# An RWKV6 layer with an MLP on one core: the first round's tensors turned by overlapping transposes, evicted by two engines

## The chip, the core and the metric

The kernel runs on one core of a Trainium2 chip. A core has five engines that matter here: TensorE (PE; its weight loads are listed as PEld), VectorE (DVE), ScalarE (ACT), GpSimd (POOL) and SyncE (SP), which only issues DMAs in this kernel. Each engine works through its own list of instructions in order and waits on semaphores for the others. The metric is the time of one execution on the device in microseconds (us), lower is better. Several runs are made of each kernel, and the median is compared.

## What is computed

The reference, cut to what matters:

```
for t in range(S):                              # S = 768 steps, B = 4, H = 8, D = 48
    kt, vt, rt, wt = k[:, :, t], v[:, :, t], r[:, :, t], w[:, :, t]
    y[:, :, t] = einsum(rt, state + outer(u * kt, vt))
    state = wt[:, :, :, None] * state + outer(kt, vt)
x = y.transpose(0, 2, 1, 3).reshape(B, S, H * D)       # 4 x 768 x 384
xn = (x - mean(x)) / sqrt(var(x) + 1e-6) * g_ln
out = x + maximum(xn @ w_ch1, 0) @ w_ch2               # 384 -> 1536 -> 384
```

All data is float32.

## The kernel before

The 768 steps of each batch are cut into two halves of 384, so there are 8 rounds (4 batches x 2 halves). A round has two units, each of four heads (`u0`, `u1` in round 0; `new` are those of the next round). A unit needs `w`, `r` and `k` with the head dimension on the partitions, 64 rows to a head, two heads (a pair) to a tile of 128 x 384: that is what `turned` (line 306) makes. For the units of later rounds it does so with three 128 x 128 transposes and one eviction by ACT. For round 0 (line 318) the data is loaded in another layout (`load_rows`, line 133: 48 numbers of a head and a step block side by side, with zeros behind the last), and each 64 x 128 piece is made by a product with the identity; two of them, for the two heads of a pair, use the left and the right half of the array's columns.

`ps_t` holds two PSUM buffers, and every `turned`, `product_sums`, `ends` and `turned_x` takes one of them; so the third piece of work in a row waits until ACT has emptied the first. `products` (line 372) multiplies r by k, and `product_sums` (line 390) sums that over a head with six products against `sel`, which holds `u`; these have 2 moving columns each. `warm(n)` (line 292) puts products of zeros on PE, n x 128 columns; nobody uses their result, the profile calls them `idle`.

The decayed products inside a block of 64 steps are built by doubling: for each of six levels, `quads` (line 416) multiplies k and r on PE, 24 products a unit, `grow` (line 436) multiplies decays into k and r in place on DVE, and `keep` (line 453) writes the new part of A on DVE. A `grow` waits for the `quads` of its level, and the next `quads` for that `grow`. Behind the levels come the states (`ends`, `states`), the outputs (`own_outputs`, `outputs`), the layer norm (`moments`, `norm`, `turned_x`) and the MLP (`mlp`), whose products are interleaved with the levels of the next rounds.

The MLP's weights are converted in 24 parts: `begin` (line 243) is three ACT operations and the fetch of a further part by SP, `join` (line 284) is `shifted` and `added`, two and one DVE operations. The first three parts must be joined before the first product of the MLP.

The order is written out by hand: each engine's instructions stand in the order in which the program issues them (`InOrder`, line 39). The prologue, lines 734 to 818, is what the change touches: turn w, r, k of u0, with a `warm(2)` behind each; level 0 of u0; turn w of u1; totals; the sums of u0; turn r, k of u1; level 0 of u1; then the loop over levels 1 to 5 (line 769), in which the tensors of round 1 are turned along the way, with a `warm(3)` in levels 1 to 4.

Of the kernel before, what the change touches and what calls it, by code (L numbers as in the profile page):

```python
# [9 lines left out]
F32 = mybir.dt.float32  # L10
# [5 lines left out]
ALU = mybir.AluOpType  # L16
# [36 lines left out]
def kernel(  # L53
# [13 lines left out]
    PE, ACT, DVE, POOL, SPO = (  # L67
        InOrder(tc, e) for e in (nc.tensor, nc.scalar, nc.vector, nc.gpsimd, nc.sync)
    )
    SP = nc.sync  # L70

    B, H, S, D = r.shape
    P = 128
    HP = 64
# [4 lines left out]
    TT = 3  # L79
    RN = TT * P  # L80
# [3 lines left out]
    W = NK * P  # L84
    NLEV = 6
# [5 lines left out]
    pairs = range(NP)  # L91
# [4 lines left out]
    p2 = ctx.enter_context(tc.tile_pool(name="p2", bufs=2))  # L96
    p3 = ctx.enter_context(tc.tile_pool(name="p3", bufs=3))
# [24 lines left out]
    def load(q, which="wkr", eng=SP):  # L122
        for nm in which:
            for c in range(TT):
                eng.dma_start(
                    out=nat[nm][q % 2][:, c, :, 0:D],
                    in_=steps({"w": w, "k": k, "r": r}[nm], q, c),
                )

    def flat(nm, q):  # L130
        return nat[nm][q % 2].rearrange("p c h d -> p (c h d)")
# [33 lines left out]
    for j in range(2):  # L165
        ACT.dma_start(
            out=sel[ds(HP * j, D), :, j], in_=u.rearrange("(r j) d -> j d r", j=2)[j]
# [4 lines left out]
    ident = const.tile([P, P], F32, name="ident")  # L172
# [18 lines left out]
    for lev in range(NLEV - 1):  # L191
# [3 lines left out]
        for base, sign in ((0, 1), (n - 1, -1)):  # L195
            POOL.affine_select(
                out=m, in_=m, compare_op=ALU.is_ge, fill=0.0, base=base,
# [10 lines left out]
        out=bits0, in0=masks[0].rearrange("p q n -> p (q n)"), scalar1=-1.0, scalar2=None,  # L208
# [34 lines left out]
    def begin():  # L243
        nonlocal begun
        i = begun
        if i < len(parts) and i - joined < (len(held) if i < len(held) + LOW else LOW):
            words = raw.pop(i)
            lo, hi = words[:, :, 0].bitcast(U32), words[:, :, 1].bitcast(F32)
            if i < len(held):
                rest[i] = held[i].bitcast(I32)  # L250
            else:
                rest[i] = low.tile([P, WC], I32, tag="rest", name=f"rest{i}")
            upper = rest[i].bitcast(F16).rearrange("p (n two) -> p n two", two=2)[:, :, 1]
            ACT.activation(out=parts[i][0], in_=hi, func=AF.Abs, scale=2.0**-16)
            ACT.activation(out=rest[i], in_=lo, func=AF.Copy, scale=2.0**-29)
            ACT.activation(out=upper, in_=hi, func=AF.Copy, scale=2.0**-100)
            begun = i + 1
            fetch()
# [25 lines left out]
    def join():  # L284
        shifted()
        added()
# [5 lines left out]
    def warm(n, tag="m"):  # L292

        while n > 0:
            m = min(n, RN // P)
            ps = (ps_m if tag == "m" else ps_t).tile([P, RN], F32, tag=tag, name="idle")
            PE.matmul(
                ps[:, 0 : m * P], nought.broadcast_to([P, P]), nought.broadcast_to([P, m * P]),
                start=True, stop=True,
            )  # L300
            n -= m
# [4 lines left out]
    def turned(q, nm, pr):  # L306
        a = st.setdefault(q, {})
        if pr == 0:
            if nm == "w":
                if q % U == 0:  # L310
                    st["w"] = p1.tile([P, U, W], F32, tag="w", name=f"wT{q // U}")
                a["w"] = st["w"][:, q % U]
            elif "rk" not in a:

                rk = a["rk"] = p4.tile([P, 2, W], F32, tag="rkT", name=f"rkT{q}")
                a["r"], a["k"] = rk[:, 0], rk[:, 1]
        ps = ps_t.tile([P, RN], F32, tag="t", name=f"{nm}_ps{q}_{pr}")
        if q < U:

            for c in range(TT):  # L320
                for j in range(2):
                    at = ((2 * pr + j) * TT + c) * D
                    PE.matmul(
                        ps[ds(HP * j, HP), ts(c, P)], flat(nm, q)[:, ds(at, HP)], ident,
                        start=True, stop=True,
                    )
            ACT.copy(
                out=a[nm][:, ts(pr, RN)].rearrange("p (m c) -> p m c", c=TT),
                in_=ps.rearrange("p (c m) -> p m c", c=TT),
            )  # L330
            return
        for c in range(TT):
            PE.transpose(
                ps[:, ts(c, P)],
                nat[nm][q % 2][:, c, ts(pr, 2)].rearrange("p j d -> p (j d)"), ident,
            )
        ACT.copy(out=a[nm][:, ts(pr, RN)], in_=ps)
# [33 lines left out]

    def products(q, eng=DVE):
        a = st[q]
        if q < U:

            a["ruk"] = [
                p3.tile([P, RN], F32, tag="xn", name=f"ruk{q}_{pr}") for pr in pairs
            ]
            for pr in pairs:
                eng.tensor_tensor(  # L380
                    out=a["ruk"][pr], in0=a["r"][:, ts(pr, RN)], in1=a["k"][:, ts(pr, RN)],
                    op=ALU.mult,
                )
        else:
            ruk = p2.tile([P, NK, P], F32, tag="kn", name=f"ruk{q}")
            ruk = ruk.rearrange("p k t -> p (k t)")
            a["ruk"] = [ruk[:, ts(pr, RN)] for pr in pairs]
            eng.tensor_tensor(out=ruk, in0=a["r"], in1=a["k"], op=ALU.mult)

    def product_sums(q):  # L390
        b, f, g = units[q]
        a = st[q]
        ps = ps_t.tile([P, RN], F32, tag="t", name=f"own_ps{q}")
        for pr in pairs:
            for c in range(TT):
                PE.matmul(
                    ps[:, ts(pr * TT + c, 2)], a["ruk"][pr][:, ts(c, P)],
                    sel[:, NP * g + pr], start=True, stop=True,
                )
        o = a["own"] = p4.tile([P, TT, NH], F32, tag="own", name=f"own{q}")  # L400
        ACT.copy(
            out=o.rearrange("p c (r j) -> p r c j", j=2),
            in_=ps[:, 0 : 2 * NK].rearrange("p (r c j) -> p r c j", r=NP, j=2),
        )
# [11 lines left out]
    def quads(q, lev):  # L416

        n = 1 << lev
        rnd, uu = divmod(q, U)
        if uu == 0:  # L420
            ps = ps_a.tile([P, 2, 512], F32, tag="a", name=f"a_ps{rnd}_{lev}")
            a_ps[rnd] = ps[:, :, 0 : W // 2].rearrange("s j (u k t) -> s j u k t", u=U, k=NK)
        K = st[q]["k"]
        R = st[q]["r"].rearrange("p (m q two n) -> p m q two n", m=NM, two=2, n=n)
        for c in range(NK):
            for i in range(2):
                for j in range(2):
                    m = 2 * c + i
                    rows = ds(HP * j, D)
                    PE.matmul(  # L430
                        a_ps[rnd][ds(C * (i ^ j), C), j, uu, c]
                        .rearrange("s (q n) -> s q n", n=n),
                        K[rows, ts(m, C)], R[rows, m, :, 1, :], start=True, stop=True,
                    )
# [280 lines left out]
    def each(f, *ranges):  # L715
        calls = [()]
        for r_ in ranges:
            calls = [c + (x,) for c in calls for x in r_]
        return [lambda c=c: f(*c) for c in calls]

    def run(tasks):
        for t in tasks:
            t()
# [12 lines left out]
    fetch(2)  # L736
    for nm in "wrk":
        run(each(turned, [u0], nm, pairs))
        warm(2)
    for nm in "wrk":  # L740
        POOL.memset(nat[nm][0][:, :, :, D:HP], 0.0)
    products(u0)
    quads(u0, 0)
    load(new[0], "wrk", SPO)
    grow(u0, 0)
    run(each(turned, [u1], "w", pairs))
    totals(0, DVE)
    warm(2)
    product_sums(u0)
    for nm in "rk":  # L750
        run(each(turned, [u1], nm, pairs))
        warm(2)
    for nm in "wrk":
        POOL.memset(nat[nm][1][:, :, :, D:HP], 0.0)
    products(u1)
# [3 lines left out]
    load_v(u0, SPO)  # L759
    load(new[1], "r", SPO)  # L760
    load_v(u1, SPO)
    load(new[1], "k", SPO)
    begin()
    begin()
    warm(3)
    grow(u1, 0)
    keep(0, 0)
    ahead = each(turned, new[:1], "wrk", pairs) + each(turned, new[1:], "wrk", pairs)
    for lev in range(1, NLEV):
        quads(u0, lev)  # L770
        quads(u1, lev)
        run(ahead[2 * lev - 2 : 2 * lev] if lev < NLEV - 1 else [])
        if lev in (2, 3):
            begin()
        warm(3 if lev < NLEV - 1 else 0)
        for which in ("rk",) if lev < NLEV - 1 else "kr":
            for q in (u0, u1):
                grow(q, lev, which)
        keep(0, lev)
# [11 lines left out]
    exchanged(u0)  # L791
    states(u1)
    product_sums(u1)
    join()
    own_term(u1, POOL)
    own_outputs(u0)
    warm(3, "t")
# [4 lines left out]
    own_outputs(u1, "m")  # L802
    outputs(u1)
    moments(0)
    begin()
    load(units_of(2)[0], "w", SPO)
    load(units_of(2)[1], "w", SPO)
    run(ahead[8:])
# [3 lines left out]
    warm(3)  # L812
    norm(0)
    begin()
    join()
    products(new[1])
    run(each(turned_x, [0], range(KC)))
# [11 lines left out]
    for rnd in range(1, NR + 1):  # L829
# [3 lines left out]
        for lev in range(NLEV):  # L833
# [22 lines left out]
            if rnd == 1:  # L856
                if lev < 2:
                    tasks += each(load, new, "kr"[lev], [SPO])
                if lev == 2:
                    SPO.dma_start(  # L860
                        out=u_bc,
# [108 lines left out]
```

## Time and profile before

| | |
|---|---|
| median of 5 runs | 586.85 us (586.53 to 591.17) |
| the profiled execution | 586.53 us, of which 584.5 us are the profile's span |
| PE busy | 572.4 us (98%), 8644 instructions |
| DVE busy | 272.6 us (47%) |
| ACT busy | 195.0 us (33%) |
| POOL busy | 90.5 us (15%) |

The profile's page lists, for one execution, the busy time of the engines (part 1), the same in 40 slices of some 14.6 us with the clock that PE was granted in tenths of full speed (part 2), and the chain of work that ended last (part 4). Answers of the trace go further: busy time in any stretch, the chain in order of time, and the instructions in order of time. A group such as `x24` holds 24 records; a float32 product leaves two records, a transpose one. A busy PE is not PE at its peak, and idle products count as busy.

### The profile page before, as it was taken

To read this page: it belongs to the slowest core of one execution; us is meant where nothing else is said; L and a number is where in the kernel's file an instruction comes from. 1 tells how busy PE (TensorE), PEld (TensorE's weight loads), DVE (VectorE), ACT (ScalarE), POOL (GpSimd) and SP (SyncE) were. 2 spreads that over 40 slices of the span, in tenths; PEclk is the share of its full clock that TensorE was granted. 3 is DMA by queue.
4 is the path that set the end of the run, shared out by engine and by line. 5 is a ranking of instruction groups with operands and counts; after the bars stand their busy time and mean duration, and the time that the engine had idled before them with its cause. 6 is when DMAs were issued, how large, how long until landed. Compare 5 with 4: busy or idle time off the path is not lost.

```text
span 584.5 us, 19224 instructions
## 1 busy us (share of the span) xinstructions
PE 572.4 (98%) x8644; PEld 383.9 (66%) x8644; DVE 272.6 (47%) x575; ACT 195.0 (33%) x426; POOL 90.5 (15%) x124
## 2 busy tenths in 40 slices
PE   9998999999999999999999999999999999999997
PEld 6776765766666666666766666666666666666554
DVE  3889799687273634343462543336254531130000
ACT  3568586412442224311432124312331015202200
POOL 6130010204340025000620008000320000000000
PEclk9999899999999999999999999999999999999999
DMA  9928895037304311340204302031000000000000
GB/s 231 187 90 169 184 246 137 6 87 137 72 14 100 73 33 25 63 91 20 57 4 91 66 29 42 2 64 28 15 3 2 15 29 2 1 15 28 0 15 27
DMA packets 114193, 36.53 MB, mean 63 GB/s; under 512 B 104768, under 2 KB 111040, under 8 KB 114112
## 3 DMA queue, kind: packets, MB, share of 16 engines
q1 hardware_dynamic: 112240, 34.72, 27.1%
q8 instruction: 68, 1.11, 0.8%
q10 hardware_dynamic: 1872, 0.59, 0.4%
q14 instruction: 13, 0.11, 0.1%
HBM read 28.51 MB, written 4.72 MB: 57 GB/s over the span
## 4 chain that ended last, share of the span: by engine, by line
PE 92%; DVE 4%; ACT 3%; issue 1%; DVEq 0%; ACTq 0%
PE o_ps L49 32%; PE h_ps L49 31%; PE a_ps L49 11%; PE y L49 4%; PE w_ps L49 2%; PE k_ps L49 2%; PE kv L49 2%; PE idle L49 2%; PE r_ps L49 2%; PE kn_ps L49 2%; PE xT_ps L49 1%; DVE w_sb L49 1%; DVE rkT L49 1%; ACT rest L49 1%; PE own_ps L49 1%
## 5 line engine op out<-in xcount | busy, mean ns | idle before, releaser
L49 PE MATMUL o_ps<-w_sb,h 128*128 128x384 f32 x576 | 199.3, 490 | 1.3 <-ACT h L49 1.0
L49 PE MATMUL h_ps<-xT,w_sb 128*128 128x384 f32 x576 | 198.3, 492 | 0.0
L49 PEld LDWEIGHTS h_ps<-xT,w_sb 128*128 128x128 f32 x576 | 105.4, 191 | 62.5 <-issue 0.5
L49 PEld LDWEIGHTS o_ps<-w_sb,h 128*128 128x128 f32 x576 | 104.3, 190 | 62.7 <-ACT h L49 2.0
L49 ACT ACTIVATE h<-h_ps 128x384 f32<-128x384 f32 x96 | 46.9, 489 | 143.8 <-PE h_ps L49 143.7
L49 DVE TENSOR_TENSOR rkT<-rkT,tot 128x768 f32<-128x768 f32 (+1 forms) x96 | 76.6, 840 | 37.2 <-issue 26.0
L49 PEld LDWEIGHTS a_ps<-rkT 48*64 48x64 f32 x4608 | 72.0, 135 | 20.8 <-issue 14.7
L49 PE MATMUL a_ps<-rkT 48*64 48x32 f32 x4608 | 77.1, 220 | 0.3 <-issue 0.3
L49 DVE TENSOR_TENSOR o<-o_ps,x 128x384 f32<-128x384 f32 x24 | 13.4, 557 | 122.4 <-PE o_ps L49 122.3
L49 POOL TENSOR_TENSOR vo<-v,own 128x576 f32<-128x576 f32 x16 | 19.2, 1198 | 289.8 <-DVE own L49 249.8
L49 DVE SCALAR_TENSOR_TENSOR s<-s,decay,kv 128x48 f32<-128x48 f32 x160 | 29.3, 258 | 34.3 <-PE kv L49 34.2
L49 DVE COPY_PREDICATED A<-mask,a_ps 128x768 f32<-128x768 int8 x32 | 38.3, 1198 | 0.0
L49 DVE TENSOR_TENSOR x<-y,vo 128x288 f32<-128x288 f32 x32 | 13.1, 452 | 51.8 <-PE y L49 51.8
L49 ACT COPY rkT<-k_ps 128x384 f32<-128x384 f32 x32 | 14.3, 478 | 55.5 <-PE k_ps L49 55.5
L49 ACT ACTIVATE xT<-xT_ps,g_sb 128x384 f32<-128x384 f32 x24 | 13.6, 580 | 54.0 <-PE xT_ps L49 54.0
L49 ACT COPY rkT<-r_ps 128x384 f32<-128x384 f32 x32 | 14.6, 478 | 23.7 <-PE r_ps L49 23.7
L49 DVE TENSOR_SCALAR w_sb<-w_sb 128x384 f32<-128x384 f32 (+1 forms) x48 | 19.2, 401 | 0.8
L49 ACT COPY wT<-w_ps 128x384 f32<-128x384 f32 x32 | 14.4, 479 | 14.0 <-PE w_ps L49 8.9
L49 DVE TENSOR_REDUCE own<-rk 128x12 f32<-128x576 f32 x12 | 9.0, 750 | 20.7 <-POOL rk L49 20.6
L49 ACT ACTIVATE rstd<-mv,eps 128x3 f32<-128x3 f32 x8 | 2.4, 297 | 48.5 <-DVE mv L49 48.4
L49 DVE TENSOR_TENSOR rkT<-rkT,wT 128x768 f32<-128x768 f32 x16 | 17.8, 1146 | 0.8 <-PE a_ps L49 0.8
L49 PE MATMUL r_ps<-ident,nat_r 128*128 128x128 f32 (+1 forms) x132 | 16.2, 277 | 2.0 <-ACT rkT L49 1.9
(73 smaller groups left out, 520.3 us busy)
## 6 DMA issues: line engine op xcount, KB each, us to landing
raw<-in_moe_w_ch_dram SPq DMA_DIRECT2D x24, 384.0 KB, 4.0
v<-in_v_dram SPq DMA_DIRECT2D x48, 96.0 KB, 3.5
out_dram<-o SPq DMA_DIRECT2D x24, 192.0 KB, 2.5
nat_w<-in_w_dram SPq DMA_DIRECT2D x42, 96.0 KB, 3.4
nat_r<-in_r_dram SPq DMA_DIRECT2D x42, 96.0 KB, 2.9
nat_k<-in_k_dram SPq DMA_DIRECT2D x42, 96.0 KB, 2.8
vx<-v SPq DMA_DIRECT2D x28, 72.0 KB, 2.9
nat_r<-in_r_dram ACTq DMA_DIRECT2D x2, 288.0 KB, 5.0
```

What stands on the lines that cost most here:

```text
L49: return lambda *args, **kw: self.tc.keep_in_program_order(f(*args, **kw))
```

## The change

Five things change, all in round 0.

1. `turned` for round 0 uses PE transposes in place of products with the identity. For each block of steps and each pair it makes first a transpose of 128 columns, of which the upper 64 rows are wanted, and then one of 64 columns over the lower 64 rows, which the first had filled with other data.
2. For unit u0, the second pair's eviction goes to DVE in place of ACT.
3. `products` of round 0 is one DVE operation a unit in place of two, in a buffer of another pool.
4. All the `warm(2)` of the prologue go. The sums of u0 (`product_sums(u0)`) move from behind the totals to level 1 of the loop, where they take the place of `warm(3)`. The turning of u1's w moves ahead of u0's level 0.
5. A `begin` moves from behind `moments(0)` to level 4 of the loop; a `join` moves from ahead of u1's own term to behind the norm; the load of one k moves behind two `begin`s on SP.

```
         if q < U:
             for c in range(TT):
-                for j in range(2):
-                    at = ((2 * pr + j) * TT + c) * D
-                    PE.matmul(
-                        ps[ds(HP * j, HP), ts(c, P)], flat(nm, q)[:, ds(at, HP)], ident,
-                        start=True, stop=True,
+                for j in (1, 0):
+                    at = ((2 * pr + j) * TT + c) * D - HP * j
+                    PE.transpose(
+                        ps[0 : HP * (j + 1), ts(c, P)],
+                        flat(nm, q)[:, ds(at, HP * (j + 1))], ident,
                     )
-            ACT.copy(
+            (DVE.tensor_copy if q == 0 and pr else ACT.copy)(
...
     for nm in "wrk":
         run(each(turned, [u0], nm, pairs))
-        warm(2)
...
     products(u0)
+    load(new[0], "wrk", SPO)
+    run(each(turned, [u1], "w", pairs))
     quads(u0, 0)
-    load(new[0], "wrk", SPO)
     grow(u0, 0)
-    run(each(turned, [u1], "w", pairs))
     totals(0, DVE)
-    warm(2)
-    product_sums(u0)
-    for nm in "rk":
-        run(each(turned, [u1], nm, pairs))
-        warm(2)
+    run(each(turned, [u1], "rk", pairs))
...
-    load(new[1], "k", SPO)
     begin()
     begin()
+    load(new[1], "k", SPO)
...
-        if lev in (2, 3):
+        if lev in (2, 3, 4):
             begin()
-        warm(3 if lev < NLEV - 1 else 0)
+        if lev == 1:
+            product_sums(u0)
+        elif lev < NLEV - 1:
+            warm(3)
...
     product_sums(u1)
-    join()
     own_term(u1, POOL)
...
     moments(0)
-    begin()
     load(units_of(2)[0], "w", SPO)
...
     norm(0)
     begin()
     join()
+    join()
     products(new[1])
```

More of the change, by code (lines that the diff above doesn't have):

```diff
@@ L374, in products @@
         if q < U:
[L376 to L383, printed above, removed]
+            ruk = p2.tile([P, TT, H, D], F32, tag="x", name=f"ruk{q}")
+            ruk = ruk.rearrange("p c h d -> p (c h d)")[:, 0:W]
         else:
@@ L386, in products @@
             ruk = ruk.rearrange("p k t -> p (k t)")
-            a["ruk"] = [ruk[:, ts(pr, RN)] for pr in pairs]
-            eng.tensor_tensor(out=ruk, in0=a["r"], in1=a["k"], op=ALU.mult)
+        a["ruk"] = [ruk[:, ts(pr, RN)] for pr in pairs]
+        eng.tensor_tensor(out=ruk, in0=a["r"], in1=a["k"], op=ALU.mult)
     def product_sums(q):
```

## The prediction

> **What bounds the kernel now.** I read the chain in order of time first. For the first 24 us it is PE alone:
>
> ```profile
> 0.99 3.78 PE idle L49 x6
> 4.77 2.15 PE w_ps L49 x24
> 6.92 0.63 PE idle L49 x2
> 7.55 1.46 PE r_ps L49 x24
> 9.01 0.63 PE idle L49 x2
> 9.64 1.46 PE k_ps L49 x24
> 11.11 0.63 PE idle L49 x2
> 11.73 0.83 PE a_ps L49 x48
> ```
>
> No eviction and no DMA stands between the pieces, although r and k each wait for ACT by the program: the idle product covers the wait, or makes it. So a tensor costs 2.09 us (7.55 to 9.64), of which idle products take 0.63. Then I cut the span into stages (columns: stretch, PE busy, PEld, DVE, ACT, POOL, granted clock, DMA):
>
> ```profile
> 4.70:21.68 16.98, 16.98 (x268) 13.58 (x267) 6.44 (x12) 8.86 (x19) 6.60 (x27) 1.00 1.22 247
> 21.68:36.20 14.52, 14.11 (x513) 11.43 (x513) 13.34 (x15) 7.92 (x17) 1.63 (x2) 1.00 0.68 167
> 36.20:52.40 16.20, 14.04 (x418) 11.54 (x419) 15.45 (x53) 13.05 (x29) 5.88 (x7) 1.00 0.37 82
> 52.40:73.13 20.73, 20.73 (x242) 14.56 (x242) 17.48 (x34) 13.90 (x32) 0.00 (x0) 0.92 0.93 188
> 73.13:94.35 21.22, 18.79 (x292) 12.16 (x284) 19.81 (x35) 19.16 (x43) 2.45 (x2) 1.00 0.92 238
> ```
>
> Turning (row 1) is PE's; the levels (row 2) belong to PE and DVE about equally; states and norm are DVE's; row 4 is PE's again; row 5 is DVE's and ACT's. Behind 94 us the chain is PE's products, which the change doesn't touch. The change lies in rows 1 to 3, and what it saves must pass rows 4 and 5.
>
> Row 4 has a clock of 0.92. One stretch makes it:
>
> ```profile
> 60.77:64.19 3.42, 3.42 (x26) 3.07 (x27) 3.35 (x7) 0.34 (x2) 0.00 (x0) 1.00 1.11 275
> 64.19:67.60 3.41, 3.41 (x11) 2.30 (x10) 3.13 (x6) 1.00 (x3) 0.00 (x0) 0.50 1.19 142
> ```
>
> Asked for the sums' product alone, the first of these stretches holds
>
> ```profile
> 60.77:64.19 3.42, 2.56 (x23) 2.47 (x23) 0.34 (x2) 1.00 1.11 275
> ```
>
> So a 3.41 us window that was mostly sums (2 moving columns, "busy" while their weights load) is followed by one at half clock. By record starts, data streamed through the array for about 0.28 of it. The lowest other window, 43.71 to 47.12, has 0.53 (0.34 without transposes), and kept the clock.
>
> **The turning, on PE.** Before: 24 records a tensor, two side by side, 0.109 us a pair by their starts: 12 x 0.109 = 1.31. After: 12 transposes a tensor, one record each, none side by side. The near row is
>
> ```profile
> 23.31 0.87 PE L49 MATMUL w_ps<-ident,nat_w 128*128 128x128 f32 x6
> ```
>
> six in 0.87 with the last one's tail of 0.27 less 0.109, so 0.109 each: again 1.31. The transposes themselves gain nothing; the dropped idle products do.
>
> [...] The trace has its price: wherever 64-column products follow 128-column ones or the reverse, the start comes 0.095 us late (an idle of 0.213 us of streaming started at 9.26, the next k at 9.57; 25 of 25 switches from o_ps to a_ps are within 0.003 of it). The new code alternates 128 and 64 columns. [...] I take 0.109 and keep 0.205 as the other end.
>
> **The evictions.** ACT's take 0.478 (rows of wT and rkT). DVE's of this shape isn't in the trace: its copy of 32 x 384 from PSUM took 0.55, the low end; one DVE row took 1.88 in place of 0.99 while POOL copied, and POOL makes masks until 10.9 us, so 1.0 is the high end. I take 0.55, nearest in size. From the last start to an eviction is 0.35. A buffer's cycle is then 0.6 + 0.35 + 0.48 = 1.43 (DVE 1.50), just over PE's 1.31: evictions set the pace, at about 1.45 a tensor.
>
> In steps: w0 starts at 4.6, when the 8 first idle products end (its DMA landed at 4.40); its first eviction can't start before 6.63, when ACT's table is loaded; r0 from 7.1, k0 8.55, u1's w 10.0 to 11.5, u0's quads to 12.4, r1 from 12.5, k1 13.9, its evictions end at 16.0; before it was 20.0. On DVE: u0's products 10.8 to 11.7, grow from 12.5, totals (2.65) to 16.2, u1's products (0.96 in one, before 1.21 in two) to 17.1, grow to 18.0. Before, that grow ended at 21.93. **Gain 3.9.** With evictions of 1.0 it is 3.1. DMAs don't stop it: r0, k0, u1's tensors had landed by 4.8, 6.1 and 8.6, and round 1's w and r by 12.8 and 15.8, needed at 19 and 22. SP issues in the same order up to two fetches; the moved k load waits behind them (some 1 us) and is needed only behind 40 us.
>
> **Level 1.** Sums (12 x 0.111 = 1.34) take the place of warm(3) (0.65): PE's step from 3.08 to 3.75, plus one switch. DVE there is 0.8 us behind PE because of the 1.88 row, so part is covered; in levels 4 and 5 DVE waits for PE (0.79 at 32.5). **Cost 0.4**, bounds 0 and 0.75. Their eviction on ACT is 0.17, behind w's. The products' new buffers are those of x, which is first written at 45 us, when u0's sums have long been read: nothing.
>
> **The moved begin and join.** A begin is 1.7 us of ACT. From 45.92 to 47.46 PE waited for ACT, which was in two begins ahead of r's evictions; one is gone, PE gains 1.5 there. At level 4 it lies in ACT's idle (ACT 7.92 of 14.52), ahead of kn's eviction, which was released 0.5 us after it could have ended; if that cover is gone it costs up to 0.5. The join (1.25 of DVE) isn't saved: it moves from 43.2 to behind the norm. The norm comes some 1.3 earlier, the last of three joins ends at about 52.1 as it did (52.2). The first h product then starts at 51.5 relative to before, in place of 52.4, with the third part joined before its third weight is needed. **Gain 0.9**, bounds 0 and 1.3. PE carries it to 73 us, where DVE had been idle for 2.5 us.
>
> Sum without the clock: 3.9 - 0.4 + 0.9 = **4.4 us**.
>
> **The clock.** Where a low window falls depends on 3.41 us steps, counted from the rise at 6.16 us in this profile (product starts halve their distance there). In level 1 the new order runs 1.4 us of sums, then quads that stream 0.45 of their time: the window 19.8 to 23.2 comes to about 0.31, between the lost 0.28 and the kept 0.53. I think it is lost (chance 0.65). Half clock for 3.41 us is 1.7 us of PE; DVE covers a little: **cost 1.2**. Then the shift is 3.2 us, u0's and u1's later sums start at 57.3, and fall into the window 57.35 to 60.77: that loss stays. If level 1 keeps the clock, the shift of 4.4 splits those sums over two windows, and 1.5 more is gained.
>
> [...] The second is a narrow fit; I give it 0.17. [...]
>
> **The rivals.**
> - Likeliest (0.45): 4.4 - 1.2 = 3.2 from the profiled execution's 586.53, 583.3. The median of the runs shown is 0.3 above that execution, within noise; I put 583.3.
> - Clock kept in level 1, and later sums split (0.20): 4.4 + 1.5 = 5.9, 580.6.
> - Switches paid (0.10): w0 ends 7.7, each tensor 2.46, k1's last eviction 21.5 against 20.0: costs 1.5 + 0.4, gains 0.9, 587.5. [...]
> - Evictions slow, cover lost at kn, no gain at the norm (0.10): 3.1 - 0.75 - 0.5 - 1.2 = 0.7, 585.9.
> - The other side: transposes don't count (0.15). [...]
>
> A measurement of this kernel tells from no change what exceeds about 0.5%, 2.9 us. Faster by that: most of the first case, the second: 0.56. Within: the rest of the first, switches, slow evictions, the mild form of the last: 0.29. Slower: 0.15. The range from 579.8 to 588.5 leaves out the fastest ends of the second case and the last one.
>
> **What would show it.** Starts of the transposes 0.109 apart (0.205: switches; 0.213: half clock). k1's eviction done near 16, u1's first grow near 18. A half-clock row at about 23 to 27, and at 61 to 64. The first h product 4 to 5 us earlier than 52.4. The forecast is wrong if the clock falls before 16 us, if DVE's evictions take 1 us, or if the gain at 52 is gone at 94.

## The result, and the profile after

The changed kernel takes 586.49 us in the median of 43 runs (582.6 to 589.5), the kernel before 588.38 in 80 runs beside it (584.65 to 593.32). The ratio is 0.9961, 95% interval 0.9946 to 0.9976: faster by 0.4%, some 2.3 us by the ratio and 1.9 by the medians, where the prediction had 583.3 us. The profiled execution of the changed kernel took 588.74 us, of which 587.0 are the span.

**The prologue is as predicted.** This is the chain in order of time (columns: start, duration, what) in the changed kernel, from the second tensor on:

```profile
7.22 1.53 PE r_ps L49 x12
8.75 1.53 PE k_ps L49 x12
10.28 1.53 PE w_ps L49 x12
11.80 0.83 PE a_ps L49 x48
12.63 1.46 PE r_ps L49 x12
14.09 1.46 PE k_ps L49 x12
15.55 0.02 issue
15.57 0.49 ACT rkT L49
```

No idle product stands between the tensors; one follows the other after 1.53 us on the chain where it was 2.09, and k's last eviction ends at 16.06 (predicted: near 16.0). By the starts the transposes are 0.109 us apart. The first u1 `grow` on VectorE ends at 18.2, where before it was 21.93.

**Then the lead is lost.** Here are stretches of the changed kernel, cut at the same events as those of before (columns: stretch, PE, PEld, DVE, ACT, POOL busy, granted clock, DMA share, GB/s):

```profile
4.60:18.10 13.50, 12.39 (x216) 10.14 (x218) 7.75 (x13) 7.70 (x16) 6.66 (x28) 1.00 1.24 270
18.10:36.24 18.14, 17.90 (x460) 14.83 (x455) 12.82 (x14) 8.80 (x20) 1.53 (x2) 0.72 0.74 163
36.24:52.36 16.12, 15.03 (x461) 12.34 (x454) 14.35 (x51) 12.31 (x27) 5.87 (x7) 1.00 0.40 93
52.36:75.73 23.37, 23.37 (x276) 16.43 (x274) 19.61 (x39) 15.22 (x36) 0.00 (x0) 0.85 0.76 180
75.73:94.15 18.42, 17.17 (x245) 10.95 (x244) 17.05 (x32) 15.95 (x35) 2.31 (x2) 1.00 0.81 226
```

The turning has become 3.5 us shorter (16.98 to 13.50), but the levels took 18.14 us where before they took 14.52, at a mean clock of 0.72. The stretch from the first h product on took 23.37 in place of 20.73, at 0.85 in place of 0.92. In this profile the granted clock stays the same for 17.07 us from its first rise, then for 10.24, 30.72 and 6.83: five, three, nine and two times 3.41. Steps of 3.41 us from that rise are called windows here. Cut by them, the same kernel shows:

```profile
18.44:21.86 3.42, 3.18 (x82) 2.89 (x79) 3.42 (x4) 1.66 (x5) 0.00 (x0) 1.00 0.78 115
21.86:25.27 3.41, 3.41 (x101) 3.35 (x94) 2.62 (x4) 0.18 (x2) 1.53 (x2) 0.50 0.93 169
25.27:28.69 3.42, 3.42 (x70) 2.34 (x71) 1.05 (x3) 2.34 (x5) 0.00 (x0) 0.50 0.99 281
28.69:32.10 3.41, 3.41 (x48) 2.59 (x44) 2.63 (x3) 1.33 (x4) 0.00 (x0) 0.50 0.67 164
59.40:62.82 3.42, 3.42 (x100) 3.38 (x94) 3.21 (x10) 2.39 (x6) 0.00 (x0) 1.00 0.90 222
62.82:69.64 6.82, 6.82 (x19) 4.59 (x19) 6.48 (x11) 1.96 (x5) 0.00 (x0) 0.50 0.60 135
```

The clock falls where the prediction put it, behind a window that holds u0's sums, and again behind one with the later sums. But the first drop lasts three windows, 10.24 us, and the second two, where the prediction had counted one each. The sums' own share of the two windows in which the clock was lost is read by asking for their product alone:

```profile
18.44:21.86 3.42, 1.50 (x12) 1.41 (x12) 0.12 (x1) 1.00 0.78 115
59.40:62.82 3.42, 2.36 (x21) 2.36 (x22) 0.17 (x1) 1.00 0.90 222
```

PE counts as busy for 3.18 and 3.42 us of these windows. Worked out from each record's columns, at the 0.109 us of 128 of them, data streamed through the array for 0.37 and 0.23 of them only.

Once the clock is down, the levels are TensorE's alone. This is the chain through two of them at half clock and into the first at full clock:

```profile
21.70 2.57 PE a_ps L49 x96
24.27 1.47 PE r_ps L49 x6
25.75 1.28 PE idle L49 x2
27.03 2.72 PE a_ps L49 x96
29.74 1.47 PE k_ps L49 x6
31.21 1.15 PE idle L49 x2
32.36 1.53 PE a_ps L49 x96
```

A level takes 5.33 us there (21.70 to 27.03, 27.03 to 32.36) and 2.98 behind it (32.36 to 35.34). TensorE has no pause in these windows; it is VectorE that waits for it, 2.37 us ahead of one `grow`. But the `quads` stream for only 0.78 and 0.66 of their time in these two levels, where the turning and the idle product behind the first stream for 0.94.

**How many windows are lost differs from run to run.** Each run has its granted clock (to three digits) and span, so the number of windows at half clock, the lost windows, follows: (1 - clock) x span / 0.5 / 3.41, rounded. The first rise of the clock, from which the windows are counted, came at 6.16 us in the profile of before and at 4.79 in that of the changed kernel, so the same code falls into windows in different ways. Mean times in us by that number (runs in brackets; before: the runs taken beside the experiments, which have their clocks on record; rows of five and more left out):

| half-clock windows | before | after | before less after |
|---|---|---|---|
| 0 | 586.4 (2) | 583.1 (5) | 3.3 |
| 1 | 587.0 (22) | 584.4 (1) | 2.6 |
| 2 | 588.9 (21) | 585.0 (9) | 3.8 |
| 3 | 589.9 (15) | 586.1 (8) | 3.8 |
| 4 | 591.8 (14) | 587.7 (13) | 4.1 |
| all, with mean number | 589.2, 2.3 (77) | 586.5, 3.1 (44) | 2.7 |

At equal numbers of lost windows the changed kernel is about 3.9 us faster (the rows with eight runs or more on both sides). It loses 0.8 windows more than the kernel before, at 1.2 (after) to 1.5 us (before) each: 3.9 less 1.1 is 2.8, and the means show 2.7. The runs in the two columns weren't taken together, and the kernel before itself differs by some 0.5 us between one set of runs and another at equal numbers, so the 3.9 is good to about half a microsecond. And the profiled execution of before, from which all was reckoned, was one of those with a single window, 586.53 us against a mean of 589.2.

### The profile page after: what moved, and what is told of

It reads as the page before. It is cut to its first block, busy times and chain, and to the rows that moved or that the text cites. A ratio compares the mean times of both kernels' runs of the same rounds, so it can differ in the third digit from the quotient of the medians.

```text
span 587.0 us, 19053 instructions
## 1 busy us (share of the span) xinstructions
PE 574.6 (98%) x8558; PEld 385.8 (66%) x8558; DVE 272.1 (46%) x576; ACT 193.9 (33%) x423; POOL 91.8 (16%) x124
## 3 DMA queue, kind: packets, MB, share of 16 engines
q1 hardware_dynamic: 112240, 34.72, 26.4%
## 4 chain that ended last, share of the span: by engine, by line
PE 91%; ACT 5%; DVE 2%; issue 1%; DMA 1%; ACTq 0%; DVEq 0%
PE o_ps L49 32%; PE h_ps L49 30%; PE a_ps L49 11%; PE y L49 4%; PE kv L49 2%; PE k_ps L49 2%; PE r_ps L49 2%; PE w_ps L49 2%; PE kn_ps L49 2%; ACT rest L49 2%; PE xT_ps L49 1%; PE own_ps L49 1%; ACT rkT L49 1%; PE idle L49 1%; DVE w_sb L49 1%
## 5 line engine op out<-in xcount | busy, mean ns | idle before, releaser
L49 PEld LDWEIGHTS a_ps<-rkT 48*64 48x64 f32 x4608 | 74.1, 138 | 20.8 <-issue 14.0
L49 PE MATMUL a_ps<-rkT 48*64 48x32 f32 x4608 | 79.3, 222 | 0.1
L49 PE MATMUL r_ps<-ident,nat_r 128*128 128x128 f32 x108 | 16.7, 285 | 2.5 <-ACT rkT L49 1.5
L49 PEld LDWEIGHTS r_ps<-ident,nat_r 128*128 128x128 f32 x108 | 13.0, 142 | 8.1 <-issue 2.4
```

Of the source, the lines that this page charges most:

```text
L49: return lambda *args, **kw: self.tc.keep_in_program_order(f(*args, **kw))
```

## The experiments

Three theories were set against each other. CLOCK: the windows thinned out by the sums cost the gain, by their number. WORK: the change moved TensorE's work to where it is the bound, and what it won ahead of VectorE and ScalarE they don't carry on. FETCH came up with the first results: pauses of TensorE that no wait explains, at fixed places of its instruction list. The experiments were measured in four sets, each with the kernel before beside it: 589.94 us in the first (e1, e3, e4, e5), 588.65 in the second (e6 to e9), 588.64 in the third (e10 to e12), 588.97 in the last. At one, two and three lost windows the kernel before is 0.2, 0.7 and 0.4 us longer in the first set than in the second, so a difference of some 0.5 us between kernels of these two sets isn't shown.

**e1: u0's sums split over two levels, with the idle products kept.**

```
-        if lev == 1:
-            product_sums(u0)
-        elif lev < NLEV - 1:
+        if lev in (1, 2):
+            product_sums(u0, pairs[lev - 1 : lev])
+        if lev < NLEV - 1:
             warm(3)
```

> The changed kernel, with u0's sums cut in two: three products in level 1 and three in level 2, each followed by the warm(3) of before. Theory CLOCK (the gain of the prologue is given back by half-clock windows that the sums open): no half-clock row between 18 and 33 us, levels 1 to 5 some 3 to 4 us shorter than in the changed kernel's profile (18.1 to 36.2 us for DVE), some 1.5 us off the mean time of the changed kernel, ratio to before about 0.993. Rival WORK (the gain is lost to work and waits at full clock): PE gets 1.2 us more in levels 1 and 2, so no gain or 0.5 us longer than the changed kernel, ratio 0.996 to 0.998.

584.44 us (582.99 to 585.88), 0.9896 of before (0.9861 to 0.9931). In the profile the half clock in the levels is gone; the one behind the later sums is still there (60.0 to 66.8). The edit does two things, it splits the sums and keeps the idle product beside them; which of the two the clock needed isn't shown.

**e3: the later sums apart.** The sums of round 1's second unit are made a level later; u0's stay as in the change.

```
-                if lev == 1:
-                    tasks += each(product_sums, now)
+                if lev in (1, 2):
+                    tasks += each(product_sums, now[lev - 1 :][:1])
```

> The changed kernel, with the sums of round 1's second unit one level later (level 2 of round 1), so that 2.8 us of sums no longer stand in one piece at 60 us. CLOCK: no half-clock row at 60 to 70 us, the one at 22 to 32 stays; 1 to 2 us off the changed kernel, ratio about 0.9935. WORK: same products, only moved, no difference: ratio 0.996.

583.81 us (583.26 to 584.83), 0.9893 (0.9861 to 0.9925). In the profile there is no half clock at 60 to 70 us, and one window at 23.0 to 26.4: that window followed one that streamed 0.38.

**e4: both.**

> Both of these edits. CLOCK: full clock in all or nearly all runs, the spread of the runs falls from 7 to about 1 us, the time is 580 to 582.5, ratio 0.988 to 0.991. WORK: the spread falls, but the time stays at the best runs of the changed kernel plus the added idle products, 583 to 585, ratio 0.993 to 0.996.

583.69 us, 0.9889 (0.9857 to 0.992), and the spread of the six runs is 1.0 us (583.24 to 584.24) where that of the changed kernel is 6.9. Five of the six had no half-clock window. The ratio is in the range of CLOCK, the time in that of WORK. The profile's row of the clock, ahead of which that of the changed kernel is set:

```profile
PEclk9799799999999999999999999999999999999999
```

```profile
PEclk9999999999999999999999999999999999999999
```

**e5: the kernel before with the later sums apart**, the edit of e3 alone.

> The kernel before, with the sums of round 1's second unit one level later. It gives the time of the old prologue without the half-clock rows near 60 us. CLOCK: about 2 us under before (1 to 3 windows less a run), 585 to 586.5, ratio 0.995 to 0.997; the whole change is then worth the distance to the version with both edits, 4 to 5 us. WORK: that distance is 1 to 2 us only.

586.55 us (584.21 to 589.45), 0.9949 (0.992 to 0.9977), with 1.3 half-clock windows in the mean where the kernel before has 2.3. So a good part of what e3 and e4 gain over the change can be had without it; e4 is still 2.9 us below e5. Fewer lost windows aren't all of it: at none, one, two and three e5 is 1.7, 1.3, 1.4 and 1.1 us below the kernel before of its own set (one to five runs each). What else the later sums save isn't shown.

CLOCK is borne out: with no work taken away (e4 even has idle products added), the changed kernel becomes 2.8 us faster (0.9889 of before where it had 0.9961) and steady. But at no half-clock window e4 takes 583.7 (5 runs), the changed kernel 583.1 (5) and e5 585.05 (3): there the change is worth 1.4 to 2 against e5, not 4.4. At one and two windows e3 is 2.4 and 3.2 below e5 (583.5 and 584.5 against 585.9 and 587.7, three to five runs each). In e4's profile the lead over e5 is 2.9 us at the first h product (51.09 against 54.03), 2.0 at the first long piece of o products on the chain (91.52 against 93.55), and 0.85 at the sixth group of those (115.82 against 116.67). The first loss is WORK's. In e4 VectorE's joins stand on the chain from 67 us on:

```profile
66.35 0.66 ACT held L49
67.02 0.84 DVE w_sb L49 x2
...
68.38 0.84 DVE w_sb L49 x2
...
69.74 0.56 DVE w_sb L49
70.30 1.74 DVE rkT L49 x2
72.03 0.90 DVE A L49
```

where e5's chain is PE's up to 75.5. Behind the norm's joins VectorE's list is the same in both; once TensorE comes earlier, VectorE is what is late. This is read from the two chains and wasn't tried by itself.

The second loss is a pause. In the changed kernel the chain has at that place

```profile
112.22 4.07 PE o_ps L49 x12
116.28 2.40 PE y L49 x153
118.68 0.93 issue
119.61 0.79 PE y L49 x39
120.41 2.13 PE o_ps L49 x6
```

with PE waiting for nothing that the profile shows. The kernel before has a shorter piece of this kind, behind the y products:

```profile
114.61 2.94 PE y L49 x192
117.55 1.17 PE o_ps L49 x3
118.72 0.34 issue
```

In the changed kernel, e1, e3 and e4 the pause comes at one and the same record of TensorE, number 4289 (counted from 0, its waits on semaphores included), at 113 to 119 us; in the kernel before and e5 there is none there, and a shorter one (0.34 and 0.18) 256 records later. The profile's list of queues has one that brings instructions:

```profile
q8 instruction: 67, 1.10, 0.8%
```

67 packets of 16 KB. TensorE has 17208 records in this profile (loads, products and waits), 257 to a packet, and 17380 in that of before, which has 68 packets: 256 to a packet. And the long pauses of e4 stand at records 1217, 1985, 2241, 4289: each 193 past a multiple of 256. That is FETCH. The packets' own times in the trace fit it: in the changed kernel one starts at 117.40 and takes 0.96 us, and the pause ends at 119.61, 1.25 us after it has landed. In the six profiles with a pause at record 4289 (also e6 and e8) it ends 1.24 to 1.56 us after such a landing.

**e6: e4 with the begin and the join where they were.**

```
-        if lev in (2, 3, 4):
+        if lev in (2, 3):
             begin()
...
+    join()
     own_term(u1, POOL)
...
     moments(0)
+    begin()
...
     begin()
     join()
-    join()
```

> The e4 kernel (u0's sums split over levels 1 and 2, each followed by warm(3); round 1's second sums a level later) with the begin and the join put back where they were before the change. MOVE (the prediction's step): the move is worth 0.9 us; the first h product then starts 0.9 us later than e4's 51.1, at about 52.0, and the whole is 0.9 us longer: 0.9905 of before where e4 had 0.9889. COVER (rival): in e4 the chain from 63 to 84 us is VectorE's (joins, rkT, A), and VectorE has the same joins behind it by then in either order; the lead at the first h product goes by the first o_ps group (e4: 89.6 us), and the whole is within 0.3 us of e4.

583.81 us (582.69 to 588.21), 0.9927 (0.9897 to 0.9957). At no half-clock window it takes 583.05 (5 runs), 0.6 less than e4, of which the two sets may make some 0.5: the move, priced at a gain of 0.9, shows no gain that lasts, as COVER had it. In the mean, though, e6 is 0.9 longer than e4 (584.67 against 583.77), because half its runs lost the clock; in its profile the window 42.86 to 46.28 streamed 0.42 and was followed by half clock. TensorE waits there for 1.13 us until ScalarE, which is in two `begin`s, has emptied a buffer; in e4, with one of them moved away, that wait is 0.24.

**e7: e4 with small products ahead of the norm**, which only shift what comes later in TensorE's list.

```
     warm(3)
+    ps = ps_m.tile([P, RN], F32, tag="m", name="pad")
+    for _ in range(32):
+        PE.matmul(
+            ps[0:2, 0:2], nought.broadcast_to([P, 2]), nought.broadcast_to([P, 2]),
+            start=True, stop=True,
+        )
     norm(0)
```

> The e4 kernel with 32 products of 2 x 2 (64 records on TensorE, nothing else) put in ahead of the norm at some 47 us, where TensorE waits for VectorE. FETCH: TensorE gets its instructions in blocks of 16 KB, and block ends fall every 256 of its records (193 past a multiple of 256). A block that passes in less time than the next one takes to come (some 2.5 us from the fetch) ends in a pause: e4 pauses 1.0 us at record 4289, inside the 192 short y products at 114 us, where the kernel before has its block end in slow products. With 64 records ahead, record 4289 falls at the start of the y group, behind 4 us of long o_ps products: no pause over 0.3 us there, o_ps #5 to #6 takes 7.2 us in place of 8.2, and the whole is about 0.9 us shorter than e4: 0.9874 of before. PLACE (rival): the pause belongs to the y group itself (a wait that the profile doesn't show): it stays, and the whole is as e4, 0.989, or a little longer by the 0.5 to 1 us of the added products if VectorE isn't the cover.

They came to 128 records, not 64: e7's profile has 19185 instructions where e4's has 19057, two loads and two products for each. The pause is gone:

```profile
108.32 4.07 PE o_ps L49 x12
112.39 2.94 PE y L49 x192
115.33 2.13 PE o_ps L49 x6
```

and the fifth to the sixth o group takes 7.01 us where e4 has 8.18. So the pause belongs to the place in the instruction list, not to the y products. The whole gained only 0.1 in the median: 583.56 us (582.11 to 585.43), 0.9905 (0.9868 to 0.9942), because the small products themselves (1.74 us in which hardly anything streams) thin out the window at 47.6 to 51.0 to 0.33 with half clock behind it in the profile; five of the six runs lost one or two windows. The single run without took 582.11, 1.6 below e4's mean of 583.68 at none, which the two sets explain for some 0.5.

**e8: u0's sums back in the prologue**, idle products in all levels, the later sums apart.

> The changed kernel with u0's sums put back into the prologue (behind the totals), warm(3) in all levels from 1 to 4, and round 1's second sums a level later, as in e3 and e4. CLOCK: no window of 3.41 us in level 1 holds mostly sums or idle; in the prologue the sums (1.34 us) stand between transposes, and the window's share stays over 0.5: full clock from the first rise to the end, spread within 1.5 us, time within 0.5 us of e4 (0.989 of before). If the prologue's window falls under 0.4, one to three half-clock windows there, each 1.2 us. WORK (rival): TensorE was the bound of the prologue, so the sums cost their 1.34 us there again and save only 0.77 in levels 1 and 2: 0.6 us longer than e4, 0.990, with k1's last eviction at 17.4 in place of 16.06.

584.86 us (583.12 to 585.87), 0.9921 (0.9891 to 0.9951), 0.6 half-clock windows in the mean, none in the profile; at none 584.0 (4 runs), 0.4 above e4, and more if the sets are allowed for. VectorE's first u1 `grow` starts 1.3 us later than in e4 (18.44 against 17.13): WORK has it right here, the sums cost their time where TensorE is the bound.

**e9: e4 with the old products on half columns** in place of the transposes.

```
-                for j in (1, 0):
-                    at = ((2 * pr + j) * TT + c) * D - HP * j
-                    PE.transpose(
-                        ps[0 : HP * (j + 1), ts(c, P)],
-                        flat(nm, q)[:, ds(at, HP * (j + 1))], ident,
-                    )
+                for j in range(2):
+                    at = ((2 * pr + j) * TT + c) * D
+                    PE.matmul(
+                        ps[ds(HP * j, HP), ts(c, P)], flat(nm, q)[:, ds(at, HP)], ident,
+                        start=True, stop=True,
+                    )
```

> The e4 kernel with the change's turning undone and all else kept: two products side by side on half the columns again, in place of the transposes that overlap; evictions still by two engines, no idle products between. The prediction says that the transposes themselves gain nothing and the dropped idle products do: k1's last eviction still ends at 16.0 to 16.3 and the first h product starts within 0.3 us of e4's 51.1. DRAIN (rival, for the transposes): if pairs of half columns are slower where they alternate without idle products, a tensor takes over 1.6 us in place of 1.45, and the prologue ends 0.9 us or more later. FETCH, besides: these products leave 144 more records on TensorE than the transposes, so that record 4289 falls ahead of the y group: no pause of 1 us there, and the whole is 0.9 us shorter than e4, 0.9874 of before.

The prologue says that the transposes gain next to nothing: tensors start 1.48 us apart (7.39, 8.87, 10.35) where it was 1.44, and VectorE's first u1 `grow` starts at 17.52 against 17.13, of which 0.30 was there from VectorE's first eviction on (6.73 against 6.43). The y group has no pause (7.01 us again). Yet the kernel takes 588.9 us (582.78 to 590.58), 0.9991 (0.9958 to 1.0023). The 144 more records put a block's end, record 705, into level 1:

```profile
17.82 1.61 PE a_ps L49 x96
19.43 0.59 PE w_ps L49 x4
20.02 1.79 issue
21.81 0.44 PE w_ps L49 x2
```

and its window and what follows are

```profile
19.18:22.60 3.42, 1.63 (x31) 1.35 (x24) 3.42 (x4) 1.10 (x3) 0.00 (x0) 1.00 0.86 130
22.60:36.25 13.65, 13.65 (x218) 10.53 (x218) 5.85 (x7) 3.88 (x11) 0.84 (x2) 0.50 0.63 149
```

PE was busy for 1.63 of 3.42 us; four windows at half clock followed. Ten of the twelve runs lost four to six windows, the two that lost none took 583.2. So a pause of 1.8 us thinned out a window, half clock followed, and the median is 5 us above e4's. That the window would have kept the clock without the pause is read from e4, whose levels did; it wasn't tried apart.

**e10: the changed kernel with 24 of the small products** of e7, and nothing else.

> The changed kernel itself, with 24 products of 2 x 2 (4 records each, 96 on TensorE) ahead of the norm at some 47 us, and nothing else. FETCH: the pause of 1.1 us at record 4289 inside the y products goes, o_ps #5 to #6 takes 7.0 us in place of 8.2; the added products cost up to 1.2 us ahead of the first h product, of which VectorE's joins from 63 to 84 us cover most. The clock is as in the changed kernel (3 half-clock windows a run in the mean), so the mean is 0.5 to 1.2 us below its 586.5, and lower at each number of half-clock windows (583.1 at none, 585.0 at two, 587.7 at four). NO FETCH (rival): the pause stays or turns up elsewhere, and the mean is equal or up to 1 us longer.

585.6 us (582.49 to 588.48), 0.9941 (0.991 to 0.9971); mean 585.5 against the changed kernel's 586.5, which lies in what FETCH expected. No pause at the y group (7.02 us). At two and three half-clock windows it is 0.4 and 0.1 below the changed kernel (4 and 6 runs), and it lost 2.75 of them in the mean, not 3.1: of the 1.0 us a part is the clock's, and what the pause alone costs this kernel isn't settled: these differences are no larger than those between sets.

**e11: e4 with the idle products cut into pieces of 128 columns**, and **e12: the same for e8**; both have `warm(6)` ahead of the norm.

```
     def warm(n, tag="m"):
         while n > 0:
-            m = min(n, RN // P)
+            m = 1
...
-    warm(3)
+    warm(6)
     norm(0)
```

> The e4 kernel with every idle product of 384 columns cut into three of 128 (the same streaming, 12 records in place of 4: some 70 more by the y group, without the cost of the padding), and idle products of 768 columns in place of 384 ahead of the norm. FETCH and CLOCK together: the y group starts at record 4053 or a little behind, its block ends fall 236 records in and behind its end, no pause over 0.7 us there; no half-clock window in most runs: about 582.3 to 582.8, 1 us below e4. Rival: the records added in the levels move block ends into short products there (1217 and its neighbours, where e4 already pauses 1.0 us), one pause is only exchanged for another, and the time is e4's 583.7 or above.

> The e8 kernel (u0's sums in the prologue as before the change, round 1's second sums a level later) with the same cutting of the idle products and 768 columns of them ahead of the norm. FETCH and CLOCK: no pause at the y group, 1 us below e8 at the same number of half-clock windows (584.0 at none), so about 583.0; the idle products ahead of the norm keep the window there over 0.5. Rival (WORK): the sums cost in the prologue what they save in the levels, and the pauses only change places: 584 to 585 as e8.

584.46 us (583.15 to 586.31), 0.993 (0.9903 to 0.9957), and 585.68 (583.87 to 589.04), 0.9951 (0.9925 to 0.9977): the rivals are right (e12 is even above its rival's 584 to 585). The y group has no pause in either, but record 1217, in the levels, has a longer one than in e4 (1.06 us from record to record). This is e11's chain there, 1.60 by that measure:

```profile
29.33 1.28 PE a_ps L49 x76
30.61 1.38 issue
31.99 0.54 PE a_ps L49 x17
```

with half clock from 32.69 to 36.10 behind it; e12 has 1.96 at the same number, and half clock behind it too. One pause was exchanged for another.

**e13: e4 with twice 12 small products**, each beside an idle product (at 41 and 47 us).

> The e4 kernel with twice 12 small products (96 records in all): behind the idle product ahead of u0's outputs at 41 us, and ahead of the idle product before the norm at 47 us. Meant as a version that beats both kernels. FETCH: no pause at the y group (o_ps #5 to #6 7.0 us in place of 8.2), the idle products behind the small ones keep the window there over 0.5: at full clock 582.5, 1.2 below e4 at the same number of half-clock windows, and 0.990 of before or less in the median. Rival: the small products (0.026 us a record, nothing streamed) thin out the windows at 41 to 50 us, the clock drops there for one or two windows in most runs, and the mean is e4's 583.7.

583.41 us (582.66 to 586.34), 0.9914 (0.9884 to 0.9944); 583.0 at none and at one half-clock window (2 runs each), 585.7 at two (3). No pause at the y group; the profile's half clock is at 60.0 to 63.5. The mean, 584.2, is no better than e4's 583.8. By the median, e4, e7 and e13 are level, some 3 us below the changed kernel and 5 to 6 below the kernel before; e4 is the steadiest.

## Why the prediction was wrong, point by point

- **The turning: right.** 0.109 us from transpose to transpose, no price for the change of width: all 66 changes between 128 and 64 columns within the six tensors start 0.109 us behind the transpose before. The rival "switches paid" is out; its 2.46 a tensor were 12 x 0.205, and no run shows 0.205 between transposes. Why these don't pay the 0.095 of the other changes of width isn't shown. Evictions took 0.48 on ACT and 0.56 on DVE, a tensor 1.44 us by the starts; k's last eviction ended at 16.06 (16.0), u1's `grow` at 18.2 (18.0). Gain by then: 3.7 to 3.9 us (3.9). e9 shows that it comes from the dropped idle products and the second evicting engine, hardly from the transposes.
- **Transposes count for the clock: right.** The windows 4.79 to 8.20 and 8.20 to 11.62 hold nothing but transposes, for 0.62 and 0.85 of their time, and the clock stayed at 1.00. The rival in which they don't count (chance 0.17, in the list 0.15) is out: in the changed kernel the clock first fell at 21.86 us, behind the window with u0's sums; that transposes cost it, no run shows. Nor does one show whether they would raise it.
- **"Half clock for 3.41 us is 1.7 us of PE; DVE covers a little: cost 1.2": this step failed, in the number of windows.** The place was right, and 1.2 us for one window is right too (1.2 a window by the runs of the changed kernel). But the thin window was followed by three at half clock, not one. TensorE was never idle in them; with the `quads` in them the first two streamed 0.81 and 0.80, and half clock went on, the third 0.86, and full clock came behind it. And it is VectorE that waits for TensorE in them (2.37 us ahead of one `grow`). VectorE's first `grow` of level 1 starts 3.73 us ahead of before (18.98 against 22.71), that of level 5 0.74 behind (36.24 against 35.50). That the later loss would stay as it was (one window) failed in the same way: two.
- **One execution taken for the kernel.** The sum was made against a run with one half-clock window, and the five runs shown (median 586.85) were faster than the kernel's 80 (588.38): that it met a fast one was chance. The prediction counted two for the changed kernel; its runs have 3.1 in the mean and 0 to 5 singly, those of before 2.3. That is 1.1 windows, about 1.3 us, of the 3.2 by which 583.3 was too low. At two windows the changed kernel takes 585.0, 1.7 above the forecast: 0.5 of this is that the profiled run of before was faster than others with one window (586.53 against 587.0), and about 0.6 that the work saved 3.8 at two windows and not 4.4. The remaining 0.6 fits a second window of before that costs 1.9 (587.0 to 588.9), where 1.2 was reckoned, and isn't shown by itself.
- **"Gain 0.9" for the begin and the join: not so.** The first h product did start early for the state of the levels (52.36, though VectorE was 0.7 late at level 5), but at full clock e6, which undoes the move, takes 583.05 where e4 takes 583.68: no gain of 0.9 is left. In the mean the move is worth 0.9, and e6's lost windows (1.2 a run, e4's 0.2) are where that shows.
- **Level 1, "cost 0.4":** not measured by itself as work; splitting the sums and adding the idle products back (e1, e4) was worth far more through the clock than it cost TensorE.
- **"Behind 94 us the chain is PE's products, which the change doesn't touch": wrong.** It doesn't touch them, but it takes 172 records out of TensorE's list ahead of them, and with that a block's end falls into the y products: 0.93 us of pause at 118.7 where before had 0.34. No step had this.

## What to carry to other kernels

Before a gain on TensorE is summed up, take the runs' granted clocks and count the half-clock windows; compare kernels at equal numbers and measured together, and price a change in how full the windows are with as many half-clock windows as profiles show, not with one: here one to four behind a thin window. A group of products with few moving columns is worth splitting, as the later sums were (in e3 the half clock at 60 to 70 us was gone), and worth watching where TensorE waits for another engine (1.13 us in e6, in a window that streamed 0.42 with half clock behind it). When the clock is whole and short products follow one another, look for pauses at fixed records: adding instructions far ahead moved them here (e7, 128 records: no pause in the y group), and put one into level 1 with half clock behind it (e9, 144 records, 1.79 us); taking 172 out, as the change does, put one of 0.93 us into the y products.

## What the runs showed of the hardware

- In the profiles of before and after every stretch between two changes of the granted clock is a whole number of times 3.41 us: 58.03, 3.41 and 515.41 before, 17.07, 10.24, 30.72, 6.83 and 518.83 after. Outside the full clock of 1.00 it was 0.50 in both.
- Shares of streaming are estimates, worked out from the records' columns at the 0.109 us that 128 of them take at full clock and twice that at half clock; they are good to some 0.03. Half clock followed windows that streamed for 0.28 of their time (before, 60.77 to 64.19), 0.37 and 0.23 (after, 18.44 to 21.86 and 59.40 to 62.82), 0.38 (e3), 0.42 (e6) and 0.33 (e7). Up to 579 us the other windows at full clock of before and after streamed for 0.53 (before, 43.71 to 47.12), 0.54 (after, 38.92 to 42.34) or more, and full clock followed. But it also followed at the end of the changed kernel behind 581.64 to 585.06, which streamed 0.38. So a share that divides the two isn't shown.
- Full clock came back behind half-clock windows that streamed 0.99 (before, 64.19 to 67.60), 0.86 and 1.00 (after, 28.69 to 32.10 and 66.23 to 69.64), and not behind those of 0.81, 0.80 and 0.77 (after, 21.86 to 28.69 and 62.82 to 66.23). Behind one thin window half clock lasted one window (before), two and three (after) and four (e9, 22.60 to 36.25).
- The sums, with 2 moving columns, keep PE "busy" for 0.111 us a record by their starts, the small products of e7 for 0.027 (64 in 1.74 us), while next to nothing streams: PE was busy for 3.42 of the 3.42 us of the window 59.40 to 62.82 (after), which streamed 0.23. The profile's busy time doesn't tell.
- The queue of instructions moved 67 packets of 16 KB for 17208 records of TensorE (after) and 68 for 17380 (before). In the changed kernel it was 1.13 us from record to record at 4289, in the y group, and the pause ended 2.21 us after the start of the packet at 117.40 (the 2.5 that FETCH expected in e7 was an estimate); at 1217, in the levels, it was 0.49 (before), 1.06 (e4), 1.60 (e11) and 1.96 (e12). In e7, e9 and e10 the y group had no pause (7.01, 7.01 and 7.02 us from o group to o group, where e4 has 8.18).
